# An attention unit of one 64-token chunk of four batches instead of four chunks of one batch

## The chip, the cores and the metric

The kernel runs on one core of a Trainium2 chip. The metric is the device time of one execution in microseconds (us). The engines named below are PE (TensorE; PEld is its weight load), DVE (VectorE), ACT (ScalarE), POOL (GpSimd) and SP (SyncE, which here only issues DMAs). "L634" is line 634 of the kernel before; lines of the kernel after are named as such.

## The reference

Four batches of 768 tokens pass a linear attention with eight heads of 48 features, then a two-layer network with 2048 hidden features. The attention keeps one 48 x 48 state for each batch and head and goes through the tokens in order:

```
for t in range(S):
    cur = einsum('bhd,bhe->bhde', u * k[t], v[t])
    y[t] = einsum('bhd,bhde->bhe', r[t], state + cur)
    state = w[t] * state + einsum('bhd,bhe->bhde', k[t], v[t])
...
h = x @ w_in                      # x: y of all heads, 3072 x 384
g = where(h >= 1, h, where(h <= -1, 0, (h + 1)**2 / 4))
out = g @ w_out
```

So the batches are independent of each other, and within a batch each token needs the state that the token before it left. The result is 3072 x 384, float32.

## The kernel before

**Attention units.** Tokens are worked on in units of `UT` = 256. There are `NU` = 12 units, and a unit is four chunks of `C` = 64 tokens. In the kernel before the four chunks of a unit follow each other in one batch, so a batch is three units (`third = u % UB`), and units 0, 3, 6 and 9 begin a batch. `attention(u, when)` does one unit:

- DMAs bring the decays `wq`, the rows of r and k `rk`, the values `vn` and, from unit 3 on, `nk`.
- DVE scans multiply up the decays inside each chunk, forwards (L487) and backwards (L482). r and k are multiplied by the results (L558, L508), and the product of a whole chunk goes to `ptot` (L505).
- PE multiplies r by k inside each chunk (`among`, L528). DVE copies the wanted half of that square into `r_` (`picked`, L534).
- PE transposes k (`ktrans`, L567), ACT copies it to `kt` (L574), and PE forms the update of the state by each chunk (`umat`, L589) in two banks `bu`. Chunk c = 2 * c2 + g has its update for four pairs of heads in 192 columns of bank `bu[g]`.
- `chain` steps the state through the chunks, one after the other: at the start of a batch one multiplication by `ptot` (L605), else an addition (L607) and a multiplication (L608), each of 192 columns. In unit 0 (`CHAINED`) PE adds the old state in PSUM instead (`add_up`, L612). `st` has six buffers of one chunk's state.
- y is summed in two banks `by`, in two parts of small matmuls at one line, L634: `cross` takes half of the products of r with the states, and `along` the other half and the products of `r_` with v. A chunk at the start of a batch has nothing before it, so its products are left out. Between `cross` and `along` ACT reads one number of each bank (`look`, L678).
- In units 0 and 1 (`ALONE`) the fourth head of each half is spread over spare rows by PE (L717), by way of an ACT copy (L722). ACT and DVE then write y to `x` as a high part (L698) and a low part (L696, or in unit 1 PE L708 and ACT L694).

**The network.** Two units make a block of 512 tokens; there are six blocks. A step (`products`) is one block with one of 16 slices of 128 hidden features: nine matmuls into a bank `hp` (`product_in`, L1226), the gate on ACT, DVE, ACT and DVE (L1038 to L1043), nine matmuls into the three banks `acc` (`product_out`, L1246). Block 0 takes its first five slices in halves of 256 tokens, block 1 its first 14 (`HALVES`), so that a half begins when its own unit is ready. The last block has another form (`fast`, L942). A slice's weights arrive once, packed, and are unpacked by `weight(f)`: ACT L414 and L416, POOL L418 (some on DVE), DVE L420, ACT L410 (some on DVE, L408), DVE L423.

**Banks.** Eight banks of PSUM: three shared ones (0 to 2), three `acc` (3 to 5) and two `hp` (6, 7). `take()` hands out banks for the units: the first ten from the list `ahead`, then 0, 1, 2 in turn.

**Order.** Nothing is issued where it stands. Each operation is added to a `Plan` with an estimated cost, the data that it reads and writes, and a due time from its unit's lead (`LEADS`) and what follows it in the unit. `Plan.best` simulates the engines by these costs, tries 40 variations of the order and keeps the one that ends first; `kept_warm` adds matmuls of zeros (L372) where PE would stand still. Every engine then runs its own queue in that order, so any change of costs or dependences gives a new order for the whole program.

Of the kernel before, what the change touches and what calls it, by code (L numbers as in the profile page):

```python
# [10 lines left out]
F32 = mybir.dt.float32  # L11
# [14 lines left out]
UB = S // UT  # L26
C = 64
NC = UT // C
SEG = 2 * NC * (C + 1)
HP = 64  # L30
NF = DF // 128
# [12 lines left out]

WARM = 50

USE, SPAN, COLUMN = 0.68, 3.4, 0.00168

EAGER, LATE = 16.0, 0.3
# [5 lines left out]
BACK, SHAKES, SHAKE, SEED = 4, 40, 0.7, 1  # L55

LOW = 7.499 * 2.0**-32
STATES = 6


class Plan:
# [221 lines left out]

SPLITS = {2, 7}
SIGNS = {9, 10, 12}
CHAINED = {0}
SUMS = 0.0
STEP, FIRST, PACED = 4.9, 24.0, 4.6
ROUNDS = 1
# [2 lines left out]
def attention_moe(tc, a):  # L292
# [52 lines left out]
    def op(engine, cost, due, reads, writes, emit, **kw):  # L345
        return plan.add(engine, cost, emit, due, reads, writes, **kw)
# [17 lines left out]
    for i in range(STATES):  # L364
        op("POOL", 0.1, SOON, (), [("spad", i)], lambda i=i: G.memset(st[i][:, 4 * D :], 0.0))

    def zeros(to, n, add):

# [69 lines left out]
    def attention(u, when):  # L438
        if u == EARLY:
            load((when, 40.0), u_sb, a["us"], ["us"])  # L440
        first, due = len(plan.ops), None
        third = u % UB
        early = u < EARLY
        v, vk = vn[u % 2], ("v", u % 2)

# [2 lines left out]

        def vs(i, c2, head, n):
            return v[i, c2, head * D : head * D + n]  # L450

        def pairs(s):
            return st[s][:, 0 : 4 * D].rearrange("p (a e) -> p a e", e=D)

        slot = [(2 * u + 1 - q) % 3 for q in range(2)]
        pv = p_.rearrange("p (q n) c -> p q n c", q=2)
# [106 lines left out]
        def ktrans(q, b):  # L563
# [4 lines left out]

        op("PE", 1.2, due, [("k", slot[0]), ("k", slot[1]), *both], [("b", ba[0]), ("b", ba[1])],
           lambda: among(ba, lambda q: rk[slot[q]][:, 1]))  # L570
        for q in (1, 0):
            b = take()
            op("PE", 0.4, due, [("k", slot[q]), "cst"], [("b", b)], lambda q=q, b=b: ktrans(q, b))
            op("ACT", 0.6, due, [("b", b)], [("kt", q)], lambda q=q, b=b: A.copy(  # L574
                kt[:, 2 * q : 2 * q + 2].rearrange("p a b c -> p (a b c)"), bank[b]))
# [18 lines left out]
        op("PE", 1.1, due, [("kt", 0), ("kt", 1), vk], [("b", bu[0]), ("b", bu[1])], umat)  # L594


        before = [None if third == 0 else state["st"]]

        def chain(c, old, new):
            c2, g = divmod(c, 2)  # L600
            up = bank[bu[g]][:, c2 * 4 * D : (c2 + 1) * 4 * D].rearrange("p (a e) -> p a e", e=D)
            pt = ptot[:, 16 * u : 16 * u + 16].rearrange("p (a c) -> p a c", c=NC)[:, :, c].unsqueeze(2).broadcast_to([128, 4, D])
            out = pairs(new)
            if old is None or u in CHAINED:
                V.tensor_tensor(out=out, in0=up, in1=pt, op=ALU.mult)  # L605
                return
            V.tensor_tensor(out=sm, in0=up, in1=pairs(old), op=ALU.add)  # L607
            V.tensor_tensor(out=out, in0=sm, in1=pt, op=ALU.mult)  # L608

        def add_up(c, old):  # L610
            c2, g = divmod(c, 2)
            PE.matmul(bank[bu[g]][:, c2 * 4 * D : (c2 + 1) * 4 * D].rearrange("p (a e) -> p a e", e=D), lhsT=ident, rhs=pairs(old),  # L612
                      start=False, stop=True, skip_group_check=True)

        for c in range(NC - (third == UB - 1)):
            old, new = before[-1], (state["st"] + 1) % STATES
            state["st"] = new
            if u in CHAINED and old is not None:
                op("PE", 0.5, due, [("s", old), "cst"], [("b", bu[c % 2])], lambda c=c, old=old: add_up(c, old), fresh=False)
            op("DVE", 0.35 if old is None or u in CHAINED else 0.71, due, [("b", bu[c % 2]), ("ptot", u, 0), ("ptot", u, 1)] + ([("s", old)] if old is not None else []),  # L620
               [("s", new), "sm"], lambda c=c, old=old, new=new: chain(c, old, new), port=True)
            before.append(new)

        by = [take(), take()]

# [8 lines left out]
            PE.matmul(out=bank[by[g]][HP * half : HP * half + M, lo : lo + C], start=first, stop=False, skip_group_check=True, **kw)  # L634

        def inter(g, h, pair, c2):
            s = before[2 * c2 + g]
            if s is None:
                return
            q, pr = divmod(pair, 2)  # L640
            i = slice(HP * h, HP * h + HP)
            put(g, pair, h, c2, lhsT=st[s][i, pair * D : pair * D + M],
                rhs=rk[slot[q]][i, 0, tokens(q, 0, pr, c2, g)])


# [31 lines left out]
        for g in range(2):  # L677
            op("ACT", 0.2, due, [("b", by[g])], [("look", g)], lambda g=g: A.copy(look[0:1, g : g + 1], bank[by[g]][0:1, 0:1]))  # L678
# [442 lines left out]
def general(tc, a, ident, w_hi, w_lo):  # L1121
# [65 lines left out]
    with (  # L1187
        tc.tile_pool(name="g_sb2", bufs=1) as sb,
        tc.tile_pool(name="g_ps2", bufs=1, space=PSUM) as ps,
    ):  # L1190
        with tc.For_i(0, B, 1) as b:
            for third in range(UB):
                ts = slice(third * UT, third * UT + UT)
                x = sb.tile([128, 3, UT], F32, tag="x", name=f"gx{third}")
                for h in range(2):
                    for j in range(3):
                        nc.gpsimd.dma_start(
                            out=x[64 * h : 64 * h + D, j, :],
                            in_=xd[bass.ds(b, 1), j // 2 * 2 + h, j % 2 * 64 : j % 2 * 64 + D, ts],
                        )  # L1200
                        nc.gpsimd.dma_start(
                            out=x[64 * h + D : 64 * h + 64, j, :],
                            in_=xd[bass.ds(b, 1), 2 + h, 64 + 16 * j : 80 + 16 * j, ts],
                        )
                xh = sb.tile([128, 3, UT], F32R, tag="xh", name=f"gxh{third}")
                xl = sb.tile([128, 3, UT], F32R, tag="xl", name=f"gxl{third}")
                V.tensor_copy(xh, x)
                G.tensor_tensor(out=xl, in0=x, in1=xh.bitcast(F32), op=ALU.subtract)
                o = [ps.tile([128, UT], F32, tag=f"o{j}", name=f"go{third}{j}") for j in range(3)]
                for f in range(NF):  # L1210
                    hp = ps.tile([128, UT], F32, tag="h", name=f"gh{third}_{f}")
                    product_in(nc, hp, f, xh, xl, w_hi, w_lo)
                    gh, gl = gate(nc, sb, hp, f"g{third}_{f}")
                    product_out(nc, o, f, gh, gl, w_hi, w_lo, f == 0, f == NF - 1)
                for j in range(3):
                    ob = sb.tile([128, UT], F32, tag=f"ob{j}", name=f"gob{third}{j}")
                    V.tensor_copy(ob, o[j])
                    nc.gpsimd.dma_start(out=a["out_b"][bass.ds(b, 1), third, j], in_=ob)


def product_in(nc, hp, f, xh, xl, w_hi, w_lo):
# [28 lines left out]

def layouts(r, k, v, w, u, moe_w_in, moe_w_out):
    def dt(x):
        x = x.reshape(B, 2, 2, 2, UB, UT, D)
        return x.transpose(0, 4, 1, 3, 6, 2, 5).reshape(NU, 2, 2, D, 2 * UT)
# [7 lines left out]
    nat = np.stack([r, k, v, w], axis=2).reshape(B, 4, 2, 4, S, D).transpose(0, 1, 2, 5, 3, 4)  # L1262

    def tokens(x):
        return x.transpose(0, 2, 1, 3).reshape(NU, 2, 128, DM).transpose(0, 2, 1, 3)

    nk = np.stack([tokens(r), tokens(k)], axis=3)
    ul = u.reshape(4, 2, D).transpose(1, 2, 0)
# [30 lines left out]

# [14 lines left out]
```

## Time and profile before

| what | value |
|---|---|
| median of 3 runs | 515.48 us (513.85 to 516.77) |
| profiled execution | 516.96 us |
| its span, first to last instruction | 515.3 us |
| PE busy | 501.9 us, 97% of the span |
| PEld busy | 424.0 us, 82% |
| DVE busy | 369.0 us, 72% |
| ACT busy | 306.8 us, 60% |
| POOL busy | 98.1 us, 19% |
| DMA | 54.72 MB, mean 106 GB/s |

The profiled execution is 1.48 us longer than the median, and 1.66 us of it lie outside its span. A busy time is the sum of the durations of an engine's instructions, matmuls of zeros among them. The chain that ended last goes back from the last instruction to what released each piece of work, so its rows tell which engine set the end in each stretch. A row of the chain or of the timeline begins with the start and the duration in us; "x64" is the number of instructions merged into it. Each float32 matmul with 64 x 64 operands is two records.

### The profile page before, as it was taken

To read this page: it belongs to the slowest core of one execution; us is meant where nothing else is said; L and a number is where in the kernel's file an instruction comes from. 1 tells how busy PE (TensorE), PEld (TensorE's weight loads), DVE (VectorE), ACT (ScalarE), POOL (GpSimd) and SP (SyncE) were. 2 spreads that over 40 slices of the span, in tenths; PEclk is the share of its full clock that TensorE was granted. 3 is DMA by queue.
4 is the path that set the end of the run, shared out by engine and by line. 5 is a ranking of instruction groups with operands and counts; after the bars stand their busy time and mean duration, and the time that the engine had idled before them with its cause. 6 is when DMAs were issued, how large, how long until landed. Compare 5 with 4: busy or idle time off the path is not lost.

```text
span 515.3 us, 13486 instructions
## 1 busy us (share of the span) xinstructions
PE 501.9 (97%) x5683; PEld 424.0 (82%) x5683; DVE 369.0 (72%) x670; ACT 306.8 (60%) x632; POOL 98.1 (19%) x84
## 2 busy tenths in 40 slices
PE   8989999999999999999999999999999999999994
PEld 6768988889999998877788787788878777789984
DVE  6989899997788989544988632799353457488663
ACT  4678888988854667533555643656434554474560
POOL 1774304503021120101111000210000131512000
PEclk9989999999999999999999999999999999999998
DMA  8984942447343442401434200621100100200002
GB/s 299 352 325 137 360 151 77 153 129 242 118 142 95 142 138 95 144 2 55 157 103 132 83 0 4 209 78 52 62 1 0 43 17 3 76 1 3 1 2 67
DMA packets 22053, 54.72 MB, mean 106 GB/s; under 512 B 3040, under 2 KB 9184, under 8 KB 21984
## 3 DMA queue, kind: packets, MB, share of 16 engines
q1 hardware_dynamic: 21840, 53.65, 30.6%
q8 instruction: 46, 0.75, 0.6%
q14 instruction: 23, 0.19, 0.1%
q10 hardware_dynamic: 144, 0.13, 0.1%
HBM read 47.09 MB, written 4.72 MB: 101 GB/s over the span
## 4 chain that ended last, share of the span: by engine, by line
PE 93%; DVE 4%; DMA 1%; issue 1%; SPq 0%; ACT 0%; DVEq 0%; ACTq 0%
PE h L1226 40%; PE acc L1246 34%; PE bank L634 5%; PE acc L942 3%; PE bank L942 3%; PE bank L528 3%; PE bank L589 2%; PE bank L567 2%; DMA cst<-in_consts 1%; DVE fl L420 1%; DVE y L482 1%; PE bank L372 1%; PE acc L528 0%; DVE wt L423 0%; DVE st L608 0%
## 5 line engine op out<-in xcount | busy, mean ns | idle before, releaser
L1226 PE MATMUL h<-x,wt 128*128 128x512 f32 (+1 forms) x1035 | 222.7, 363 | 2.3 <-DVE x L696 1.5
L1226 PEld LDWEIGHTS h<-x,wt 128*128 128x128 f32 x1035 | 171.2, 190 | 32.5 <-DVE x L696 1.7
L1246 PE MATMUL acc<-gh,wt 128*128 128x512 f32 (+1 forms) x594 | 131.4, 356 | 0.0
L1246 PEld LDWEIGHTS acc<-gh,wt 128*128 128x128 f32 x594 | 97.4, 188 | 16.8
L1038 ACT ACTIVATE g<-h 128x512 f32<-128x512 f32 (+1 forms) x99 | 50.8, 513 | 89.5 <-PE h L1226 88.7
L1040 DVE SCALAR_TENSOR_TENSOR g<-g,h 128x512 f32<-128x512 f32 (+1 forms) x99 | 57.1, 578 | 59.4 <-ACT g L1039 54.4
L1246 PE MATMUL acc<-gl,wt 128*128 128x512 f32 (+1 forms) x297 | 72.3, 352 | 0.0
L1043 DVE TENSOR_TENSOR gl<-g,gh 128x512 fp32r<-128x512 f32 (+1 forms) x99 | 60.3, 614 | 14.9 <-ACT gh L1042 14.6
L1042 ACT CAST gh<-g 128x512 fp32r<-128x512 f32 (+1 forms) x99 | 52.4, 534 | 26.9 <-DVE g L1040 24.2
L554 POOL TENSOR_TENSOR r<-cst,d 128x512 f32<-128x512 f32 x18 | 19.7, 1114 | 218.8 <-PE bank L634 170.4
L1246 PEld LDWEIGHTS acc<-gl,wt 128*128 128x128 f32 x297 | 50.6, 188 | 8.5
L1039 ACT ACTIVATE g<-g 128x512 f32<-128x512 f32 (+1 forms) x99 | 54.5, 550 | 2.9
L418 POOL TENSOR_SCALAR wraw<-fl 128x768 uint16<-128x768 f32 x13 | 40.8, 3151 | 54.4 <-ACT wraw L416 54.3
L487 DVE TENSOR_TENSOR_SCAN p<-wq,seeds 128x520 f32<-128x520 f32 x24 | 30.5, 1270 | 2.9 <-DMA wq<-in_w 2.1
L482 DVE TENSOR_TENSOR_SCAN y<-wq,seeds 128x520 f32<-128x520 f32 x24 | 32.0, 1333 | 0.8
L546 POOL TENSOR_TENSOR nk<-nk 128x768 f32<-128x768 f32 x9 | 17.3, 1920 | 58.0 <-DMA nk<-in_nk 49.3
L903 DVE SCALAR_TENSOR_TENSOR rk<-rk,h 128x512 f32<-128x512 f32 x16 | 11.0, 685 | 15.0 <-ACT rk L902 15.0
L534 DVE COPY_PREDICATED r<-below,bank 128x512 f32<-128x512 int32 x22 | 15.3, 730 | 6.7 <-PE bank L528 6.6
L634 PEld LDWEIGHTS bank<-rk,st 64*64 64x64 f32 (+1 forms) x656 | 12.2, 133 | 6.9 <-issue 3.7
L416 ACT ACTIVATE wraw<-wraw 128x768 uint16<-128x768 uint32 x16 | 17.4, 1086 | 0.3
L574 ACT COPY kt<-bank 128x512 f32<-128x512 f32 x24 | 13.9, 580 | 6.1 <-PE bank L567 6.1
L607 DVE TENSOR_TENSOR sm<-bank,st 128x192 f32<-128x192 f32 x37 | 13.1, 355 | 5.4 <-PE bank L589 4.1
(212 smaller groups left out, 609.5 us busy)
## 6 DMA issues: line engine op xcount, KB each, us to landing
rk<-in_rk SPq DMA_DIRECT2D x24, 512.0 KB, 4.7
wraw<-in_wbits SPq DMA_DIRECT2D x16, 768.0 KB, 7.8
nk<-in_nk SPq DMA_DIRECT2D x9, 768.0 KB, 4.5
wq<-in_w SPq DMA_DIRECT2D x24, 260.5 KB, 2.9
vn<-in_v SPq DMA_DIRECT2D x12, 384.0 KB, 5.8
fl<-in_w SPq DMA_DIRECT2D x12, 260.0 KB, 2.8
out_y<-g SPq DMA_DIRECT2D x10, 256.0 KB, 2.5
x<-last SPq DMA_DIRECT2D x60, 32.0 KB, 2.2
```

The lines of the kernel that those rows point to most:

```text
L418: op(on, 0.62 if f in SIGNS else 3.2, due, [("fl", k)], [("raw", f)], lambda: e.tensor_scalar(out=half(1), in0=s, scalar1=0.0, scalar2=327 ...
L482: V.tensor_tensor_scan(out=y_[:, ::-1], data0=w[:, SEG:0:-1], data1=sv[:, ::-1], initial=0.0, op0=ALU.mult, op1=ALU.add)
L487: V.tensor_tensor_scan(out=pv[:, q].rearrange("p n c -> p (n c)"), data0=w[:, 0:SEG], data1=sv, initial=0.0, op0=ALU.mult, op1=ALU.add,)
L634: PE.matmul(out=bank[by[g]][HP * half : HP * half + M, lo : lo + C], start=first, stop=False, skip_group_check=True, **kw)
L942: PE.matmul(bank[i][:, half * UT : half * UT + UT], lhsT=w[wi], rhs=g[gi], start=i not in opened, stop=True, skip_group_check=True)
L1038: op("ACT", c, due, [("b", 6 + hk)], [("g", gk)], lambda: nc.scalar.activation(gs, hs, AF.Relu, scale=0.5, bias=0.5))
L1039: op("ACT", c, due, (), [("g", gk)], lambda: nc.scalar.activation(gs, gs, AF.Square))
L1040: op("DVE", 0.13 + 0.53 * k, due, [("b", 6 + hk)], [("g", gk)], lambda: nc.vector.scalar_tensor_tensor(out=gs, in0=gs, scalar=1.0, in1=hs, ...
L1042: op("ACT", c, due, [("g", gk)], [("gh", gk)], lambda: nc.scalar.copy(ghs, gs))
L1043: op("DVE", 0.15 + 0.5 * k, due, [("g", gk), ("gh", gk)], [("gl", gk)], lambda: nc.vector.tensor_tensor(out=gls, in0=gs, in1=ghs.bitcast(F ...
L1226: nc.tensor.matmul(hp, lhsT=wx[f][:, cs], rhs=xt[:, j, :], start=n == 0, stop=n == 8)
L1246: nc.tensor.matmul(o[j], lhsT=wx[f][:, cs], rhs=gt, start=first and i == 0, stop=stop and i == 2, skip_group_check=True)
```

## The change

A unit becomes one chunk of 64 tokens of all four batches. Unit u holds tokens 64 u to 64 u + 63 of every batch, so that chunk c of a unit now belongs to batch c. The four chunks of a unit do not depend on each other; each depends on the same chunk of the unit before.

- The chain through the chunks is gone, with `add_up` and `CHAINED`. A step of the state is now one operation for the two chunks in bank `bu[g]`, 384 columns wide: in unit 0 one multiplication by `ptot`; in units 1 to 10 an addition of the old state (`step`) and a multiplication in place (`fade`), for g = 0 and 1.
- The states are two buffers, one that a unit reads and one that it writes, in turn.
- y of a unit takes its states from the unit before. Unit 0 has none of these products: `cross` and `look` are left out there, and half of `along`.
- Unit 11 hands nothing on: its transposes of k, their copies, `umat` and the step are left out.
- The list `ahead` ends in banks 5 and 2 where it ended in 3 and 4 (these are `by` of unit 0), and the turn of the shared banks begins one earlier.
- The host lays out r, k, v and w in the new order and puts the result's tokens back. Shapes and bytes are the same.
- The scratch for DMA descriptors is set to 8192 bytes (`SCRATCH`). `general`, which runs only when the inputs' decays are out of range, writes its output by the new order.

```diff
-STATES = 6
...
-CHAINED = {0}
...
-    st = tiles(STATES, [128, 4 * D + 16], F32, "st")
-    sm = one([128, 4, D], F32, "sm")
+    st = tiles(2, [128, 2, 2, 4 * D + 16], F32, "st")
...
-    state = {"bank": 2, "st": 0}
+    state = {"bank": 1}
-    ahead = [3, 4, 5, 6, 0, 1, 7, 2, 3, 4]
+    ahead = [3, 4, 5, 6, 0, 1, 7, 2, 5, 2]
...
+        goes_on = u < NU - 1
         for q in (1, 0):
-            b = take()
-            op("PE", 0.4, due, [("k", slot[q]), "cst"], [("b", b)], lambda q=q, b=b: ktrans(q, b))
...
+            if goes_on:
+                b = take()
+                op("PE", 0.4, due, [("k", slot[q]), "cst"], [("b", b)], lambda q=q, b=b: ktrans(q, b))
...
-        bu = [take(), take()]
+        bu = [take(), take()] if goes_on else []
...
-        for c in range(NC - (third == UB - 1)):
-            old, new = before[-1], (state["st"] + 1) % STATES
-            state["st"] = new
-            if u in CHAINED and old is not None:
-                op("PE", 0.5, due, [("s", old), "cst"], [("b", bu[c % 2])], lambda c=c, old=old: add_up(c, old), fresh=False)
...
+        old, new = (u - 1) % 2, u % 2
...
+        def step(g):
+            up = bank[bu[g]][:, 0 : 8 * D].rearrange("p (c a e) -> p c a e", c=2, e=D)
+            if u == 0:
+                V.tensor_tensor(out=heads(new, g), in0=up, in1=faded(g), op=ALU.mult)
+            else:
+                V.tensor_tensor(out=heads(new, g), in0=up, in1=heads(old, g), op=ALU.add)
+
+        def fade(g):
+            V.tensor_tensor(out=heads(new, g), in0=heads(new, g), in1=faded(g), op=ALU.mult)
+
+        if goes_on:
+            op("PE", 1.1, due, [("kt", 0), ("kt", 1), vk], [("b", bu[0]), ("b", bu[1])], umat)
+            for g in range(2):
+                op("DVE", 0.5, due, [("b", bu[g]), ("ptot", u, 0), ("ptot", u, 1)] + ([("s", old, g)] if u else []), [("s", new, g)],
+                   lambda g=g: step(g))
+                if u:
+                    op("DVE", 0.47, due, [("ptot", u, 0), ("ptot", u, 1)], [("s", new, g)], lambda g=g: fade(g), port=True)
...
         def along():
-            crossed(0)
+            if u:
+                crossed(0)
...
-        ss = [("s", s) for s in before if s is not None]
+        ss = [("s", old, g) for g in range(2)] if u else []
...
-        op("PE", 0.6, due, ss + [vk, ("r", slot[0]), ("r", slot[1])], [("b", by[0]), ("b", by[1])], cross, fresh=not alone)
+        if u:
+            op("PE", 0.6, due, ss + [vk, ("r", slot[0]), ("r", slot[1])], [("b", by[0]), ("b", by[1])], cross, fresh=not alone)
...
-        op("PE", 1.65, due, ss + [("R", 0), ("R", 1), vk, ("r", slot[0]), ("r", slot[1])],
+        op("PE", 1.65 if u else 1.1, due, ss + [("R", 0), ("R", 1), vk, ("r", slot[0]), ("r", slot[1])],
```

More of the change, by code (lines that the diff above doesn't have):

```diff
@@ L28 @@
 NC = UT // C
+assert NC == B and NU * C == S
 SEG = 2 * NC * (C + 1)
@@ L45 @@
 WARM = 50
+SCRATCH = 8192
 USE, SPAN, COLUMN = 0.68, 3.4, 0.00168
@@ L363, in attention_moe @@
     last_f = ob[:, 0:UT]
-    for i in range(STATES):
-        op("POOL", 0.1, SOON, (), [("spad", i)], lambda i=i: G.memset(st[i][:, 4 * D :], 0.0))
+    for i in range(2):
+        op("POOL", 0.1, SOON, (), [("spad", i)], lambda i=i: G.memset(st[i][:, :, :, 4 * D :], 0.0))
     def zeros(to, n, add):
@@ L570, in attention @@
            lambda: among(ba, lambda q: rk[slot[q]][:, 1]))
+        goes_on = u < NU - 1
         for q in (1, 0):
-            b = take()
-            op("PE", 0.4, due, [("k", slot[q]), "cst"], [("b", b)], lambda q=q, b=b: ktrans(q, b))
-            op("ACT", 0.6, due, [("b", b)], [("kt", q)], lambda q=q, b=b: A.copy(
-                kt[:, 2 * q : 2 * q + 2].rearrange("p a b c -> p (a b c)"), bank[b]))
+            if goes_on:
+                b = take()
+                op("PE", 0.4, due, [("k", slot[q]), "cst"], [("b", b)], lambda q=q, b=b: ktrans(q, b))
+                op("ACT", 0.6, due, [("b", b)], [("kt", q)], lambda q=q, b=b: A.copy(
+                    kt[:, 2 * q : 2 * q + 2].rearrange("p a b c -> p (a b c)"), bank[b]))
             if q:
@@ L592, in umat @@
                             )
[L594 to L613, printed above, removed]
-        for c in range(NC - (third == UB - 1)):
-            old, new = before[-1], (state["st"] + 1) % STATES
-            state["st"] = new
-            if u in CHAINED and old is not None:
-                op("PE", 0.5, due, [("s", old), "cst"], [("b", bu[c % 2])], lambda c=c, old=old: add_up(c, old), fresh=False)
-            op("DVE", 0.35 if old is None or u in CHAINED else 0.71, due, [("b", bu[c % 2]), ("ptot", u, 0), ("ptot", u, 1)] + ([("s", old)] if old is not None else []),
-               [("s", new), "sm"], lambda c=c, old=old, new=new: chain(c, old, new), port=True)
-            before.append(new)
+        old, new = (u - 1) % 2, u % 2
@@ new lines, in heads, with faded @@
+        def heads(s, g):
+            return st[s][:, :, g, 0 : 4 * D].rearrange("p c (a e) -> p c a e", e=D)
+        def faded(g):
+            return ptot[:, 16 * u : 16 * u + 16].rearrange("p (a c g) -> p c g a", c=2, g=2)[:, :, g].unsqueeze(3).broadcast_to([128, 2, 4, D])
+        def step(g):
[4 more added lines that the diff above has]
+                V.tensor_tensor(out=heads(new, g), in0=up, in1=heads(old, g), op=ALU.add)
@@ L636, in inter @@
         def inter(g, h, pair, c2):
-            s = before[2 * c2 + g]
-            if s is None:
-                return
             q, pr = divmod(pair, 2)
             i = slice(HP * h, HP * h + HP)
-            put(g, pair, h, c2, lhsT=st[s][i, pair * D : pair * D + M],
+            put(g, pair, h, c2, lhsT=st[old][i, c2, g, pair * D : pair * D + M],
                 rhs=rk[slot[q]][i, 0, tokens(q, 0, pr, c2, g)])
@@ L670, in cleared @@
                           skip_group_check=True)
-        ss = [("s", s) for s in before if s is not None]
+        ss = [("s", old, g) for g in range(2)] if u else []
         if alone:
             op("PE", 0.5, due, ["zero"], [("b", by[0]), ("b", by[1])], cleared)
-        op("PE", 0.6, due, ss + [vk, ("r", slot[0]), ("r", slot[1])], [("b", by[0]), ("b", by[1])], cross, fresh=not alone)
-        for g in range(2):
-            op("ACT", 0.2, due, [("b", by[g])], [("look", g)], lambda g=g: A.copy(look[0:1, g : g + 1], bank[by[g]][0:1, 0:1]))
-        op("PE", 1.65, due, ss + [("R", 0), ("R", 1), vk, ("r", slot[0]), ("r", slot[1])],
+        if u:
+            op("PE", 0.6, due, ss + [vk, ("r", slot[0]), ("r", slot[1])], [("b", by[0]), ("b", by[1])], cross, fresh=not alone)
+            for g in range(2):
+                op("ACT", 0.2, due, [("b", by[g])], [("look", g)], lambda g=g: A.copy(look[0:1, g : g + 1], bank[by[g]][0:1, 0:1]))
+        op("PE", 1.65 if u else 1.1, due, ss + [("R", 0), ("R", 1), vk, ("r", slot[0]), ("r", slot[1])],
            [("b", by[0]), ("b", by[1])], along, fresh=False)
@@ L1217, in general @@
                     V.tensor_copy(ob, o[j])
-                    nc.gpsimd.dma_start(out=a["out_b"][bass.ds(b, 1), third, j], in_=ob)
+                    nc.gpsimd.dma_start(out=a["out_b"][bass.ds(b, 1), third, j], in_=ob.rearrange("p (c t) -> p c t", t=C))
 def product_in(nc, hp, f, xh, xl, w_hi, w_lo):
@@ L1252, in dt @@
     def dt(x):
-        x = x.reshape(B, 2, 2, 2, UB, UT, D)
-        return x.transpose(0, 4, 1, 3, 6, 2, 5).reshape(NU, 2, 2, D, 2 * UT)
+        x = x.reshape(B, 2, 2, 2, NU, C, D)
+        return x.transpose(4, 1, 3, 6, 2, 0, 5).reshape(NU, 2, 2, D, 2 * UT)
     def rows(x, fill):
@@ L1307 @@
     out = nc.dram_tensor("out_y", (DM, NT), F32, kind="ExternalOutput").ap()
-    a["out_b"] = out.rearrange("(j p) (b t c) -> b t j p c", t=UB, j=3, c=UT)
+    a["out_b"] = out.rearrange("(j p) (h c b t) -> b h j p c t", h=UB, j=3, b=B, t=C)
     a["out"] = out.rearrange("(j p) (b c) -> b j p c", j=3, c=WIDE)
@@ L1312 @@
     res = run_bass_kernel_spmd(nc, [{f"in_{n}": x for n, x in arrays.items()}], core_ids=[0])
-    return np.ascontiguousarray(res.results[0]["out_y"].T)
+    y = res.results[0]["out_y"].T.reshape(NU, B, C, DM).transpose(1, 0, 2, 3)
+    return np.ascontiguousarray(y.reshape(NT, DM))
```

8 lines of the change are left out of this document (3 added, 5 removed).

## The prediction

> **What bounds the kernel now.** I read the page first: busy shares, slices, and the chain that ended last.
>
> ```profile
> PE 501.9 (97%) x5683; PEld 424.0 (82%) x5683; DVE 369.0 (72%) x670; ACT 306.8 (60%) x632; POOL 98.1 (19%) x84
> PE   8989999999999999999999999999999999999994
> DVE  6989899997788989544988632799353457488663
> PE 93%; DVE 4%; DMA 1%; issue 1%; SPq 0%; ACT 0%; DVEq 0%; ACTq 0%
> ```
>
> PE sets the end for 93% of the span. But a busy PE also counts matmuls of zeros, so the next view is busy time in two stretches, once for all lines and once for the zeros (L372) alone. I cut at 43.43 us, where the chain changes over to PE for good. The columns are the stretch, its length, busy time and instructions of each engine, then granted clock, DMA share and GB/s.
>
> ```profile
> 14.23:43.43 29.20, 24.63 (x487) 19.79 (x479) 26.72 (x45) 20.65 (x36) 19.86 (x7) 0.94 0.75 279
> 43.43:508.84 465.41, 465.39 (x4938) 395.13 (x4938) 332.32 (x611) 279.59 (x585) 75.56 (x60) 1.00 0.27 89
> 14.23:43.43 29.20, 7.74 (x34) 5.59 (x34) 0.94 0.75 279
> ```
>
> Two stages with two limits. From 43.43 to 508.84 PE is busy for 465.39 of 465.41 us, with no zeros: here only PE work taken away counts. From 14.23 to 43.43, the **front**, 7.74 of PE's 24.63 us are zeros, while DVE is busy for 26.72 of 29.20 us, 92%. So in the front DVE and the dependences decide. The chain in order of time (start, us, what) gives its milestones:
>
> ```profile
> 30.38 0.56 DVE x L696
> 30.99 3.67 PE h L1226 x17
> 43.43 1.32 PE h L1226 x9
> 46.24 1.27 PE acc L1246 x9
> ```
>
> Unit 0's y is complete at 30.94 (L696 ends); the network's products then begin in earnest at 30.99. By 43.43 only three half slices of the first product are done, 27 matmuls, and none of the second (46.24). The products wait for y of unit 0, then for unpacked weights, and DVE works for unit 1 in between.
>
> **The change in the PE stage: unit 11.** Its two k transposes and `umat` go. The chain there:
>
> ```profile
> 417.95 4.21 PE h L1226 x18
> 422.16 0.44 PE bank L567 x4
> 424.71 1.08 PE bank L589 x64
> 425.79 4.40 PE h L1226 x18
> ```
>
> Two transposes at 0.44 are 0.88. `umat` is 1.08, and the 18 matmuls behind it take 4.40 where 18 others take 4.21, so 0.19 more for the changeover. Sum 0.88 + 1.08 + 0.19 = **2.15 us**, all on the path, as PE has no gap there. What is late next is more PE work, so nothing gives it back.
>
> **The change in the PE stage: what is added.** Units 3, 6 and 9 get a state for their first chunk: 8 more small products each. Units 3 and 4, without and with them:
>
> ```profile
> 135.36 0.62 PE bank L634 x22
> 139.35 1.56 PE bank L634 x85
> 160.44 0.62 PE bank L634 x32
> 162.32 1.56 PE bank L634 x96
> ```
>
> `cross` takes 0.62 with three quarters of its records or all 32, `along` 1.56 with 85 on the chain or 96. The added products cost **nothing**: the rows show equal lengths. If they cost the mean of a record, 1.56 / 96 = 0.016, it would be 48 x 0.016 = 0.8; I keep that for the range.
>
> **The change on DVE.** The new operations are 384 columns wide. No state operation of that width is in the trace, but the last row below has that form, PSUM and SBUF in, 384 out:
>
> ```profile
> L607 DVE TENSOR_TENSOR sm<-bank,st 128x192 f32<-128x192 f32 x37 | 13.1, 355 | 5.4 <-PE bank L589 4.1
> L608 DVE TENSOR_TENSOR st<-sm,ptot 128x192 f32<-128x192 f32 x37 | 13.7, 370 | 1.3
> L696 DVE TENSOR_TENSOR x<-bank,x 128x384 fp32r<-128x384 f32 x20 | 10.8, 551 | 5.7 <-ACT last L698 4.7 <-ACT x L698 0.9
> ```
>
> Before: 7 multiplications (0.34, below) + 37 + 37 = 2.4 + 13.1 + 13.7 = 29.2 us. After: 2 + 20 `step` and 20 `fade`, 42 x 0.551 = 23.1. The bounds for one are 0.355 (no growth) and 2 x 0.370 (none saved); I take 0.551, the row of its width. Some 6 us of DVE time go, nearly all beside a full PE, where they are worth nothing. Only those in the front count:
>
> ```profile
> 14.88 0.72 DVE L534 COPY_PREDICATED r<-below,acc 128x512 f32<-128x512 int32 x1
> 15.48 0.34 DVE L605 TENSOR_TENSOR st<-h,ptot 128x192 f32<-128x192 f32 x1
> 35.89 1.34 DVE L534 COPY_PREDICATED r<-below,bank 128x512 f32<-128x512 int32 x2 [1.64 <-PE bank L528]
> 39.52 0.36 DVE L607 TENSOR_TENSOR sm<-bank,st 128x192 f32<-128x192 f32 x1 [0.26 <-PE bank L589]
> 42.34 0.71 DVE L608 TENSOR_TENSOR st<-sm,ptot 128x192 f32<-128x192 f32 x1
> ```
>
> Unit 1's chain holds DVE from 39.52 to 43.05, 3.53 us, and its y waits for it. Afterwards y of unit 1 needs only unit 0's states, so the four operations (4 x 0.551 = 2.2) can stand behind it. Unit 0's four multiplications, 4 x 0.34, become two of 0.551: 0.26 less. Together **3.8 us** of DVE leave the way to unit 1's y. This is the lower reading of the front.
>
> **The change in the dependences of the front.** The timeline of PE and ACT gives the upper reading:
>
> ```profile
> 21.68 1.08 PE L634 MATMUL acc<-r,vn 64*48 64x64 f32 x60
> 22.80 0.43 ACT L722 COPY ob<-acc 128x128 f32<-128x128 f32 x2 [0.64 <-PE acc L634]
> 23.12 1.60 PE L717 MATMUL acc<-ob,nk 128*128 128x128 f32 x12 [0.36 <-ACT ob L722]
> 24.41 0.47 ACT L698 CAST x<-acc 128x384 fp32r<-128x384 f32 x1
> 44.75 1.49 PE bank L634 x96
> 51.30 0.86 ACT L694 CAST x<-bank 128x384 fp32r<-128x384 f32 x2
> ```
>
> Unit 0: `along` ended at 22.76, behind the chain of states. Afterwards its y needs `r_` (15.60) and its two banks; 5 was read by `picked`, and 2 is `bu[1]`, free after both steps, 15.60 + 1.10 = 16.7. So `along` can end near 18.2, some 4.5 us earlier. The change doesn't free unit 0's y from `umat`, as it could: bank 2 holds it there. Unit 1: `along` ran at 44.75; its `r_` was ready at 37.23, so without the chain it can run 7.5 us earlier, and y (52.16 now) with it. That is the upper reading: **7.5 us**.
>
> Between 3.8 and 7.5 I take **5.0**, nearer to the lower end since DVE is 92% full. Why not all 7.5: an earlier y(0) brings g and its low part (L1040, L1043) onto the same DVE earlier, and PE gets weights only as they are unpacked (first rival). For the range I keep 0 (reordered, nothing gained) and 9.3, which is y(0) at the earliest, 30.94 - 21.6: `along` to 18.2, then some 3.4 us, an estimate from L722 to the first L698 (22.80 to 24.88), the second high part (0.47), a low part (0.55) and the waits between them, if nothing else stands on ACT and DVE before them.
>
> [...] The first `fade` operations fall among POOL's weight conversions:
>
> ```profile
> 27.55 3.22 POOL L418 TENSOR_SCALAR wraw<-fl 128x768 uint16<-128x768 f32 x1 [4.54 <-ACT wraw L416]
> 32.18 6.44 POOL L418 TENSOR_SCALAR wraw<-fl 128x768 uint16<-128x768 f32 x2 [1.41 <-ACT wraw L416]
> 42.01 3.02 POOL L418 TENSOR_SCALAR wraw<-fl 128x768 uint16<-128x768 f32 x1 [3.39 <-ACT wraw L416]
> ```
>
> The L608 at 42.34 ran under the conversion from 42.01 to 45.03 and took 0.71 instead of 0.37. It was slowed by 0.34, but it ended 2 us before the conversion. So I count a `fade` in the front at up to 0.9, and it lies behind unit 1's y: no change of the sum. [...]
>
> **Sum.** 516.96 - 2.15 - 5.0 = 509.8 us for the profiled execution. That one is 1.48 over the median of the runs shown, so against the median: 515.48 - 7.15 = **508.3 us**. About 0.5%, 2.6 us, is what a measurement can tell from no change.
>
> No transfer changes in bytes. The tail after 508.84 stays: the last block's form is untouched.
>
> **Rivals.**
>
> *The front is given back to the weights.* Slice 3's conversion on POOL ends at 30.77, slice 4's near 35.4 (second row above, half of 6.44), and unpacking goes on behind it on the full DVE. If by 43.43 PE has done slices 0 to 2 in both products, that is 3 x 2.11 = 6.3 us (half of the 4.21 row above is one product) where it had done 3 x 1.06 = 3.2; less unit 1's transposes and `umat`, which now come later (1.96). Gain 1.2 in the front: 515.48 - 2.15 - 1.2 = 512.1. For it: DVE at 92%. Against: no chain, and 7.74 us of zeros to fill.
>
> [...]
>
> *Slower: two state buffers.* `step(u)` writes the buffer that `along(u - 1)` reads, so DVE may stand for PE; behind it in its queue are L1040 and L1043, and PE waits for those. Now:
>
> ```profile
> 125.54 1.08 PE bank L589 x64
> 153.83 1.08 PE bank L589 x64
> ```
>
> `umat` of unit 3 at 125.54 comes 13.8 us before its `along` (139.35), and `umat` of unit 4 at 153.83 comes 12.9 us after that `along` ended: the wait is covered. If the new order turned this round, DVE would stand for up to 13.8 us, less two steps of products that PE has ahead, 2 x 4.21: 5.4 us lost for each such unit. It decides from the second unit on: 508.3 + 10.8 = 519.1.
>
> *All of y(0).* If the front gains 9.3: 515.48 - 2.15 - 9.3 = 504.0.
>
> **How the numbers follow.** Forecast, front 3 to 8 us: 0.58. Weights, 512.1: 0.23. Full block or a new order that gains nothing, about 514.7: 0.07. Slower, 519: 0.06. All of y(0), 504: 0.06. The range runs from 503.5 to 513.5: from the largest front (504.0) to `umat` and the transposes alone (513.3). It leaves out 514.7 and 519, 0.13 together, and a little at its ends. Faster by over 0.5% (below 512.9): the forecast, all of y(0) and two thirds of the weights, 0.79. Within 0.5%: 0.15. Slower: 0.06.
>
> **What would show it.** In the profile after: no L567 and L589 of unit 11, so 88 and 704 records instead of 96 and 768; 42 state operations near 551 ns; `cross` of units 3, 6 and 9 at 0.62; the first L1226 near 22 to 25 instead of 30.99; unit 1's `along` near 38 to 41 instead of 44.75; PE full without zeros from about 38 on and to the same distance before the end. It would be wrong if PE shows gaps after the front (the slower rival: DVE waits at the step for L634), if DVE is the chain's engine past 60 us, or if the first product starts early but zeros still fill PE to 43 (the weights).

## The result and the profile after

The kernel after takes **511.27 us** in the median of 5 runs (510.04 to 511.69), beside 515.48 (513.85 to 516.77, also 5 runs) for the kernel before: ratio 0.9915, 95% interval 0.9891 to 0.994. A second measurement, against 17 runs of the kernel before on one chip, gave 510.53 against 515.19, ratio 0.9892, 0.9868 to 0.9917. So the change is worth 4.2 to 4.7 us by the medians. The forecast was 508.3, a gain of 7.15. The mean granted clock of PE differs between executions of one kernel, and the time goes with it: of 25 runs of the kernel before, five at a clock of 0.999 took 513.97 to 514.65 us, five at 0.993 or 0.994 took 516.74 to 517.73.

The page of the kernel after, in the order in which the page before was read:

```profile
PE 496.3 (97%) x5591; PEld 418.5 (82%) x5591; DVE 365.8 (72%) x631; ACT 304.7 (60%) x628; POOL 99.0 (19%) x80
PE   7889999999999999999999999999999999999995
DVE  5999999998888979533969635967353376687653
PE 94%; DMA 1%; DVE 1%; issue 1%; POOL 1%; ACT 1%; SPq 0%; DVEq 0%
```

The profiled execution took 511.69 us, its span 510.0; PE still sets the end. The stretches, cut as before (columns: stretch, its length, busy time and instructions of each engine, granted clock, DMA share, GB/s; the last line counts the zeros at L372 alone):

```profile
14.23:43.43 29.20, 24.89 (x500) 19.37 (x501) 26.62 (x41) 19.62 (x39) 16.84 (x6) 0.88 0.72 277
34.20:503.74 469.54, 469.52 (x5097) 399.14 (x5097) 338.28 (x591) 285.07 (x593) 84.53 (x62) 1.00 0.28 91
14.23:43.43 29.20, 8.66 (x20) 4.70 (x20) 0.88 0.72 277
```

Two things are to be seen. PE is now full from 34.20 us on, where it was full from 43.43, and it ends 5.1 us earlier (503.74 instead of 508.84). But in the front, VectorE is as busy as it was: 26.62 of 29.20 us instead of 26.72. The zeros did not shrink (8.66 us instead of 7.74), and POOL did less of its weight conversions (16.84 instead of 19.86). The front was **rearranged, not relieved**. The granted clock of the stretch also fell, from 0.94 to 0.88; the section on the prediction comes back to it.

What that brought is read from the network's products done by 100 us. Both kernels have by then done the attention work of units 0 to 2 and the same 180 matmuls of 256 columns. The groups of 512-column products up to 100 us, before and after:

```profile
L1226 PE MATMUL h<-x,wt 128*128 128x512 f32 x72 | 18.3, 400 | 0.0
L1246 PE MATMUL acc<-gh,wt 128*128 128x512 f32 x31 | 8.3, 400 | 0.0
L1246 PE MATMUL acc<-gl,wt 128*128 128x512 f32 x15 | 4.3, 396 | 0.0
```

```profile
L1219 PE MATMUL h<-x,wt 128*128 128x512 f32 x72 | 18.2, 399 | 0.0
L1239 PE MATMUL acc<-gh,wt 128*128 128x512 f32 x36 | 9.5, 398 | 0.0
L1239 PE MATMUL acc<-gl,wt 128*128 128x512 f32 x17 | 4.9, 395 | 0.0
```

118 before and 125 after (126 in the profile of the second measurement). Nine take 2.10 us on the chain, so 7 are **1.63 us**: by so much the front of the kernel after is ahead. With 2.15 for unit 11 it makes 3.8, near the 4.2 of the medians. Between the two profiled executions the difference is 5.27; most of the rest, 1.5 us, lies behind 100 us in work that both have. The second product's matmuls there sum to 177.6 us for 757 records before and 174.6 for 750 after, 1.4 less than the seven account for; the change does not explain it.

### The profile page after: what moved, and what is told of

Its sections match the earlier page's. It is cut to its first block, busy times and chain, and to the rows that moved or that the text cites. A ratio compares the mean times of both kernels' runs of the same rounds, so it can differ in the third digit from the quotient of the medians.

```text
span 510.0 us, 13244 instructions
## 1 busy us (share of the span) xinstructions
PE 496.3 (97%) x5591; PEld 418.5 (82%) x5591; DVE 365.8 (72%) x631; ACT 304.7 (60%) x628; POOL 99.0 (19%) x80
## 4 chain that ended last, share of the span: by engine, by line
PE 94%; DMA 1%; DVE 1%; issue 1%; POOL 1%; ACT 1%; SPq 0%; DVEq 0%
PE h L1219 40%; PE acc L1239 34%; PE bank L628 5%; PE acc L935 3%; PE bank L935 3%; PE bank L524 3%; PE bank L587 2%; PE bank L563 2%; DMA rk<-in_rk 1%; POOL wraw L418 1%; PE bank L372 0%; PE acc L524 0%; DVE rk L504 0%; SPq L352 0%; PE bank L710 0%
## 5 line engine op out<-in xcount | busy, mean ns | idle before, releaser
L1036 DVE TENSOR_TENSOR gl<-g,gh 128x512 fp32r<-128x512 f32 (+1 forms) x99 | 62.5, 636 | 18.6 <-ACT gh L1035 17.2
L418 POOL TENSOR_SCALAR wraw<-fl 128x768 uint16<-128x768 f32 x13 | 41.4, 3188 | 53.4 <-ACT wraw L416 53.3
L478 DVE TENSOR_TENSOR_SCAN y<-wq,seeds 128x520 f32<-128x520 f32 x24 | 31.2, 1300 | 0.8
L542 POOL TENSOR_TENSOR nk<-nk 128x768 f32<-128x768 f32 x9 | 17.2, 1909 | 67.6 <-DMA nk<-in_nk 67.6
L504 DVE TENSOR_TENSOR rk<-rk,y 128x512 f32<-128x512 f32 x24 | 16.8, 701 | 1.5 <-ACT nk L494 1.4
L894 ACT ACTIVATE rk<-h 128x512 f32<-128x512 f32 x16 | 9.6, 598 | 13.8 <-PE h L1219 13.8
L554 DVE TENSOR_TENSOR rk<-rk,p 128x512 f32<-128x512 f32 x24 | 16.2, 684 | 2.1 <-DMA rk<-in_rk 1.8
L416 ACT ACTIVATE wraw<-wraw 128x768 uint16<-128x768 uint32 x16 | 17.3, 1084 | 0.2
```

The lines of the kernel that those rows point to most:

```text
L418: op(on, 0.62 if f in SIGNS else 3.2, due, [("fl", k)], [("raw", f)], lambda: e.tensor_scalar(out=half(1), in0=s, scalar1=0.0, scalar2=327 ...
L478: V.tensor_tensor_scan(out=y_[:, ::-1], data0=w[:, SEG:0:-1], data1=sv[:, ::-1], initial=0.0, op0=ALU.mult, op1=ALU.add)
L1036: op("DVE", 0.15 + 0.5 * k, due, [("g", gk), ("gh", gk)], [("gl", gk)], lambda: nc.vector.tensor_tensor(out=gls, in0=gs, in1=ghs.bitcast(F ...
```

## The experiments

Unless a run says otherwise, its kernel is the kernel after with one edit. "Products" are the 512-column ones done by 100 us, counted as above: one is 0.23 us. They tell the front alone, and of one profiled execution. From the same execution come "clock", the granted clock from 14.23 to 43.43 us, and "gap", the time that PE stands still between 100 and 500 us.

| run | median us | ratio to before, 95% interval | products | clock | gap, us |
|---|---|---|---|---|---|
| before | 515.48 | 1 | 118 | 0.94 | 0 |
| after, first | 511.27 | 0.9915 (0.9891 to 0.994) | 125 | 0.88 | 0 |
| e1, unit 11 kept | 513.47 | 0.9966 (0.9948 to 0.9984) | 130 | 0.94 | 0.48 |
| e2, another order | 511.02 | 0.9933 (0.9909 to 0.9957) | 133 | 0.94 | 0.34 |
| e3, y(1) ahead of the state | 510.50 | 0.9902 (0.9882 to 0.9921) | 130 | 0.94 | 0.30 |
| e4, y(0) in banks 3 and 4 | 514.04 | 0.9968 (0.9951 to 0.9984) | 122 | 0.88 | 1.97 |
| e5, no backward scan | 508.10 | 0.9848 (0.9815 to 0.9882) | 141 | 1.00 | 0 |
| e6, short conversions | 508.70 | 0.9851 (0.9829 to 0.9874) | 142 | 1.00 | 0.16 |
| e7, no zeros before the spread | 509.75 | 0.9869 (0.9845 to 0.9893) | 138 | 1.00 | 0.86 |
| e8, before in another order | 521.59 | 1.0085 (1.0055 to 1.0116) | 126 | 1.00 | 3.86 |
| e9, more warming | 512.65 | 0.9943 (0.9921 to 0.9966) | 123 | 1.00 | 0.98 |
| e10, e9 and e7 | 513.98 | 0.9969 (0.9951 to 0.9988) | 122 | 0.88 | 1.59 |
| e11, e3 and e7 | 511.11 | 0.9913 (0.9888 to 0.9938) | 124 | 0.82 | 0.66 |
| e12, after again | 510.53 | 0.9892 (0.9868 to 0.9917) | 126 | 0.88 | 0 |

The kernel before had a median of 515.40 beside e1 to e4, 516.50 beside e5 to e8 and 515.19 beside e9 to e12; so runs of different rows are compared by their ratios. Products and gap together account for the spans of the profiled executions: set against e12 (510.0 us), every version of the kernel after comes out within 0.4 us of what its products, its gap and, in e1, 2.15 for unit 11 give, e4 alone within 1.1. So a difference of time is not always one of the front.

### e1: unit 11 hands its state on

```diff
-        goes_on = u < NU - 1
+        goes_on = True
```

> The kernel after with the transposes of k, umat and the state step of unit 11 put back; its state is used by nothing. Step of the prediction: 2.15 us of PE path come back, so 511.27 + 2.15 = 513.4 us, with 96 records of the transposes and 768 of umat. Rival, that PE work late in the program is hidden or that the gain came from elsewhere: 511.3. Rival, that a new order alone moves the time by a microsecond or more: anything from 512 to 515.

Measured 513.47, 2.20 above the kernel after. The chain of this run has the work back, in two places (start, us, what):

```profile
418.36 0.87 PE bank L563 x8
...
421.34 1.08 PE bank L587 x64
422.42 2.30 PE h L1219 x9
```

The transposes 0.87, `umat` 1.08, and 2.30 instead of 2.10 for the products behind it: the forecast's 0.88, 1.08 and 0.19. This term holds. The durations are the firmer proof: the planner's order moved with the edit (130 products and a gap of 0.48), so that the 2.20 is not unit 11 alone, and by the ratios the distance is 2.6 us or more. Counted against e12, 2.15 and 0.48 less four products (0.93) give 1.70; the spans are 511.7 and 510.0.

### e2 and e8: the same work in another order

```diff
-BACK, SHAKES, SHAKE, SEED = 4, 40, 0.7, 1
+BACK, SHAKES, SHAKE, SEED = 4, 40, 0.7, 2
```

(In e8 the kernel before, with 3.) The planner keeps the best of 40 variations; another seed gives other variations.

> The kernel after with SEED 2 instead of 1 in the plan's variations: the same operations in another order. If the order found is no lottery: 511.3 within 0.8 us. If it is one: off by more than 1 us, and part of the 4.2 us between before and after is luck of the order.

> The kernel before with SEED 3 instead of 1: the same operations in another order. If the order found matters little: 515.4 within 1 us. If the order is a lottery of the size of the change: off by 2 us or more, and the 4.2 us between before and after are as much luck as change.

e2 has a median of 511.02, and its interval overlaps that of the kernel after: nothing that can be told apart, though it has 133 products. e8 is 0.85% slower than the kernel before. So the choice of an order alone can be worth as much as the whole change. And e8 is not slower in the front: it has 126 products there, 8 more than the kernel before in its own order and as many as the kernel after. It loses behind the front, 3.86 us in gaps, 2.9 of them where PE waits for g from VectorE (L1040); another 2.7 us of its longer span stay unexplained. So the 7 products between before and after can't be put down to the change: another order of the old work brings as many. e8 shows one such order, not how often it occurs.

### e3 and e4: y earlier by itself

In e3 the transposes of k, `umat` and the steps of unit 1 are added to the plan behind its y instead of ahead of it. In e4 y of unit 0 gets two banks that nothing of its own update uses:

```diff
-    ahead = [3, 4, 5, 6, 0, 1, 7, 2, 5, 2]
+    ahead = [3, 4, 5, 6, 0, 1, 7, 2, 3, 4]
```

> The kernel after with unit 1's transposes, umat and state step placed behind the evacuation of its y, so that the banks of its y no longer wait for the step of g = 0. Theory banks (the front gained 2 us and not 5 because y of unit 1 still waits for umat and a state step by way of the shared banks): along of unit 1 starts at 38 to 41 instead of 44.28, its y is complete near 46 instead of 51.98, and the time is 507 to 509.5 us. Theory weights (DVE and the unpacking of the weights fill the front whatever y does): y earlier, time 510.5 to 512.

> The kernel after with y of unit 0 in banks 3 and 4, which it had before, instead of 5 and 2; bank 2 is one that umat writes and the step reads. Theory banks: along of unit 0 starts before 17.0 instead of 17.61, and its y is complete 1 to 3 us before 29.78; time 509 to 510.5. Theory weights: y at the same place or earlier, time 510.5 to 512.

e3 did what it was to do. Its chain has `along` of unit 1 (here L638) at 38.16 instead of 44.28, and the correction ahead of y's low part (here L711) at 45.74 instead of 50.80:

```profile
38.16 1.49 PE bank L638 x96
...
45.74 0.28 PE bank L711 x3
```

y(1) was complete at 47.26 instead of 51.98, and the time fell by 0.13% against the first measurement of the kernel after and not at all against the second. By products, 130, the front gained about 1 us, at a clock of 0.94 instead of 0.88, which may be part of it. So **4.7 us of y(1) brought 1 us of the front at most**: the upper reading of the prediction, and the half of the lower one that rested on y(1), fall with e3.

e4 did not do what it was to do. `along` of unit 0 began at 15.72 instead of 17.61, but PE stood for 2.90 us in the middle of it, and the second low part of y(0) came behind the scans and copies of unit 1 in VectorE's queue: it was complete at 33.58 instead of 29.78, and the first product began at 35.23. VectorE was busy for 25.53 us of the front instead of 26.62. The kernel was slower, 0.9968, and 1.97 us of that are gaps behind the front. What an earlier y(0) is worth by itself, e4 does not show.

### e5, e6 and e7: relieving the front

In e5 the backward scan (L478) of units 1 and 2 isn't issued: four scans of 1.24 us. In e6 POOL's conversion (L418) of the first five slices is a memset of 0.96 to 0.98 us, so that these weights lose their signs. In e7 the planner puts no zeros between `along` and the spread of unit 0. Otherwise the order is that of the kernel after in all three.

```diff
+                if u in (1, 2):
+                    return
```

```diff
-lambda: e.tensor_scalar(
+lambda: e.memset(half(1), 0) if f < 5 else e.tensor_scalar(
```

```diff
-                if free and lack > 0.15:
+                if free and lack > 0.15 and not 16.0 < free < 20.0:
```

> The kernel after in its own order, with the backward scan of units 1 and 2 left out (DVE L478, four of 1.24 to 1.25 us in the front; k is then multiplied by values left by unit 0). 5.0 us of DVE work go from 20 to 54 us, nothing else. Theory DVE (the front is as long as the DVE work before y and the products): 2 to 5 us less, 506.3 to 509.3. Theory weights, or theory zeros: within 0.8 us of 511.3, DVE waits instead.

> The kernel after in its own order, with POOL's conversion of the signs of the first five weight slices (L418, 3.0 to 3.66 us each) replaced by a memset of the same place, so that these weights lose their signs. Theory weights (the front waits for unpacked weights): each slice is ready some 2.5 us earlier, time 507.5 to 509.5. Theory DVE: within 0.8 us of 511.3, since DVE's queue is full behind it, at most what two-input operations gain when POOL no longer runs beside them.

> The kernel after in its own order, without the matmuls of zeros between along and the spreading of unit 0 (L372, 4.30 us from 21.16 to 25.46, which the plan meant as 2.3). Theory zeros: y of unit 0 is complete 2 to 3 us earlier than 29.78 and the time is 508.5 to 510. Theory DVE or weights: y of unit 0 earlier, time within 0.8 us of 511.3.

e5 and e6 bring 141 and 142 products, 16 or 17 more than the kernel after, and lie 0.4 to 0.7% below it: to relieve VectorE or POOL in the front shortens the kernel. e5 saved 5.0 us of VectorE and brought 2 to 3.5 us. But how it shortens it is not shown, for in both the front also ran at a clock of 1.00 instead of 0.88. Over 29.20 us that is 3.5 us of clock, an estimate from these two figures, or 15 products: as much as the whole gain. e7 has 138 products, a clock of 1.00 too, and a gap of 0.86 behind the front. Its interval overlaps those of the kernel after, and e10 and e11 (below), which have the same edit beside another, show none of the gain, at clocks of 0.88 and 0.82. What e7 owes to the zeros stays open.

### e9 to e12: where the stall belongs

The profile after has a stall that the profile before does not show. In the first `along` PE stood for 2.20 us, and the view gives no releaser but "issue" (its row, 18.27 2.20, stands in the chain further below). e9 puts more small matmuls ahead of everything, so that all later instructions of PE stand further on in its stream: a stall that belongs to a place there leaves `along`, one that belongs to the data or the banks stays; e10 adds the edit of e7 to that; e11 joins e3 and e7; e12 is the kernel after, beside them.

```diff
-WARM = 50
+WARM = 88
```

> The kernel after with 88 in place of 50 of the small matmuls at L378 ahead of all attention work; order and all else as in after, nothing left out. Every later TensorE instruction stands 76 instructions (38 matmuls and their weight loads) further on in TensorE's instruction stream; the 38 fall into the wait ahead of the first ktrans at 9.27 us. In after the first along stood still for 2.20 us after 28 of its 64 matmuls, and in six kernels of seven after 24 or 28 of them. [...] Theory 'the data': the stall comes from what along reads or writes, or from its first use of these banks; it stays at 24 to 28 matmuls with 1.5 to 2.9 us, and the time stays (.9905 to .9925).

> The kernel of e9 without zeros between the first along and the first spread, as in e7; nothing left out. If the 2 us of the stall and the 4.3 us of the zeros are both on the way to y(0), this is better than e7 by up to 2 us more: ratio to before .983 to .987 (e7: .9869). If the weights of slices 0 to 2 or VectorE's work set the first products once the zeros are gone, the stall is hidden behind them and e10 equals e7 within .002.

> The kernel of e3 (unit 1's state steps behind its y) without zeros between the first along and the first spread, as in e7; nothing left out. e3 alone brought 0.13% and e7 alone 0.46% against after. If the two delays follow each other on the path (y(0) first, then y(1)), together they bring 0.6% or more: ratio to before .984 to .986, the fastest version that computes all. If VectorE's backlog sets both, they bring no more than e7 alone: .9865 to .988.

> The kernel after unchanged, beside e9 to e11, so that these can be set against it directly. Expected ratio to before .9915 as measured first (.989 to .994), with a stall of 1.5 to 2.5 us after 28 matmuls of the first along again if it belongs to the kernel and not to one execution.

The stall is in e12 too, again after 28 records of `along`. In e9 it left `along` and stands in `umat`, after 20 of its 64 records. The page's counts and the timelines, e9 first (the two PE rows, then VectorE's), then e12:

```profile
PE 495.9 (97%) x5667; PEld 418.8 (82%) x5667; DVE 364.5 (71%) x631; ACT 305.1 (60%) x628; POOL 99.7 (19%) x80
```

```profile
18.28 0.26 PE L587 MATMUL bank<-vn,kt 64*64 64x48 f32 x2 [1.65 <-issue]
```

```profile
19.23 0.56 DVE L603 TENSOR_TENSOR st<-bank,ptot 128x384 f32<-128x384 f32 x1 [1.54 <-PE bank L587]
...
30.82 0.55 DVE L689 TENSOR_TENSOR x<-acc,x 128x384 fp32r<-128x384 f32 x1
```

```profile
28.99 0.55 DVE L689 TENSOR_TENSOR x<-acc,x 128x384 fp32r<-128x384 f32 x1
```

The 38 added matmuls are 76 records (5667 instead of 5591; in float32 each is recorded twice, so `along` of unit 0 is 32 matmuls in 64 records and not the 64 that the expectation took). From the 20th record of `umat` to the 28th of `along` there are 44 of `umat`, 2 of zeros, 2 of the clearing at L661 and 28 of `along`: 76. The stall moved by exactly as many records as were put ahead of it. In all twelve profiles of a kernel after, PE had 350 matmul records behind it since the start when it stood (349 in e4). So it belongs to **a place in PE's instruction stream**, not to the data or the banks.

Moving it brought no gain: the author's estimate was a time 0 to 2.5 us lower, and e9 is slower than e12 by 2.1 us. The added matmuls did not vanish in a wait as the expectation said; the first transpose began at 11.01 instead of 9.43. And in `umat` the stall made VectorE stand for 1.54 us at the step of the state (second row), in the middle of its front. VectorE, which had been 1.5 us behind e12 at the copy ahead of it (L530, 16.98 instead of 15.46), was 3.2 behind here (19.23 instead of 16.07) and gave the last low part of y(0) at 30.82 instead of 28.99. Of the 2.1 us, 0.98 are a gap behind the front, and three products fewer are 0.7. e10, slower still, has the same stall and the same delay, and a gap of 1.59. e11 has 124 products where e7 had 138: what e3 and e7 did alone does not add up. Of the versions that compute all, none is shown to be faster than the kernel after.

## Why the prediction was right in sign and too large

**Unit 11: right.** 2.15 forecast; e1 has the three terms of the sum back at 0.87, 1.08 and 0.20, and a median 2.20 higher. The records of L563 and L587 are 88 and 704 (672 + 32), as the prediction said.

**Added products and the new state operations: right in size.** Groups of the kernel after (columns: engine, operation, shapes, count, busy us, mean ns, idle before):

```profile
L563 PE MATMUL bank<-cst,rk 128*128 128x128 f32 x88 | 14.1, 289 | 0.6 <-DVE rk L504 0.6
L587 PE MATMUL bank<-vn,kt 64*64 64x48 f32 x672 | 12.6, 220 | 0.0
L605 DVE TENSOR_TENSOR st<-bank,st 128x384 f32<-128x384 f32 x20 | 10.9, 551 | 7.3 <-PE bank L587 7.2
L608 DVE TENSOR_TENSOR st<-st,ptot 128x384 f32<-128x384 f32 x20 | 10.6, 549 | 0.0
L587 PE MATMUL h<-vn,kt 64*64 64x48 f32 x32 | 1.1, 217 | 0.0
```

551 and 549 ns where 551 was taken, and `cross` of unit 3 takes 0.63 us at 159.58. VectorE's wait for `umat` ahead of `step` sums to 7.2 us in the whole run and PE has no gap behind it: the rival of the two state buffers did not come. What the chances call the full block (514.7) no run shows: under a conversion VectorE's subtraction at L1036 took 0.71 and 0.75 us, 0.40 at its shortest, and ended 1.9 us before the conversion (last section).

**The front: the step that failed.** The prediction took 5.0 us, between a lower reading of 3.8, VectorE work that leaves the way to y of unit 1, and an upper one of 7.5. It measured 1.63 by products, 2.0 to 2.5 by the medians. The mechanism, a shorter way to both y, was hardly there: y(0) came 1.16 us earlier, y(1) 0.18, and e3 shows that even 4.7 us of y(1) bring little. Unit 0 first. The chain of the kernel after through the front, in order of time:

```profile
18.27 2.20 issue
...
21.42 0.27 ACT ob L715
...
21.79 0.81 ACT fl L414
22.62 1.08 ACT wraw L416
...
23.78 3.01 POOL wraw L418
26.81 0.96 DVE fl L420
...
28.16 0.55 DVE wt L408
28.71 0.60 DVE rk L504
29.31 0.47 DVE x L689
...
29.93 1.25 DVE y L478
...
34.20 1.19 PE bank L524 x64
...
40.73 1.25 PE acc L1239 x9
...
44.28 1.49 PE bank L628 x96
```

`along` of unit 0 started at 17.61 and ended at 21.28; without the stall of 2.20 it would have been 19.1, where the prediction had 18.2. Then the chain leaves y(0): it runs through the unpacking of a weight slice on ACT (L414, L416), POOL (L418) and VectorE (L420, L408), and the second low part of y(0) (L689, 29.31) stands behind these in VectorE's queue. y(0) is complete at 29.78 instead of 30.94. The estimate of 3.4 us from `along` to y had the condition "if nothing else stands on ACT and DVE before them"; that condition is what failed: it took 8.5 us. PE's own queue had a part in it: zeros stood ahead of the spread from 21.16 to 25.46. But in e7, without them, the spread begins at 20.79 and y(0) is complete at 28.27, only 1.5 us earlier. From 26.81 to 34.20 the chain is VectorE but for short pieces, and PE stood for 2.11 us ahead of the matmuls of 34.20.

And y(0) moved ahead held the weights up. ACT's wait ahead of its copy of y(0), and POOL's conversions, of the kernel after, and POOL's of the kernel before:

```profile
21.25 0.27 ACT L715 COPY ob<-acc 128x128 f32<-128x128 f32 x1 [3.94 <-PE bank L628]
```

```profile
14.35 6.04 POOL L418 TENSOR_SCALAR wraw<-fl 128x768 uint16<-128x768 f32 x2 [11.29 <-ACT wraw L416]
23.78 3.00 POOL L418 TENSOR_SCALAR wraw<-fl 128x768 uint16<-128x768 f32 x1 [3.39 <-ACT wraw L416]
```

```profile
13.85 9.15 POOL L418 TENSOR_SCALAR wraw<-fl 128x768 uint16<-128x768 f32 x3 [10.71 <-ACT wraw L416]
```

Before, three conversions followed each other and were done at 23.00. After, the copy of y(0) stands in ACT's queue ahead of the third slice's L414, waits 3.94 us for `along`, and the third conversion ends at 26.78, 3.8 us later. By 43.43 POOL had done one conversion less. This is the first rival, the front given back to the weights, in a form that the prediction had not named: not VectorE's load but a wait on ACT. The measured 511.27 and 510.53 lie between its 512.1 and the time by the lower reading, 515.48 - 2.15 - 3.8 = 509.5, and both are nearer to 512.1 than to the forecast of 508.3.

Unit 1: `along` ran at 44.28, not at 38 to 41. The prediction let it run as soon as its `r_` was ready. Its two banks are 1 and 2, and bank 2 is one of unit 1's own `bu`, so y(1) still waited for `umat` and the step (39.58 and 40.76), a dependence that the prediction saw for unit 0 and missed for unit 1. e3 removes it, and little comes of that.

**The granted clock, for which the sum had no term.** The front of the kernel after in stretches of 10 us (columns as in the first view of stretches; the granted clock is the third figure from the end):

```profile
14.00:24.00 10.00, 7.80 (x203) 4.94 (x202) 9.30 (x14) 5.40 (x10) 6.21 (x3) 0.88 1.03 402
24.00:34.00 10.00, 8.09 (x105) 6.38 (x103) 8.94 (x13) 8.22 (x17) 6.05 (x2) 0.95 0.77 282
34.00:44.00 10.00, 9.80 (x201) 8.79 (x201) 9.18 (x16) 6.80 (x14) 5.15 (x2) 0.83 0.33 133
```

In the front PE ran for some us at half its clock: twice in the kernel after (0.50 from 22 to 24 and from 36 to 38 us), once in the kernel before (0.50 from 32 to 34), not at all in e5 to e9. One row shows what that costs. In e8 the first products begin as in the kernel before, behind the same wait, but at full clock, and take 2.26 us where the chain of the kernel before has 3.67 at 30.99:

```profile
31.03 2.26 PE L1226 MATMUL h<-x,wt 128*128 128x256 f32 x17 [1.48 <-DVE x L696]
```

Over 29.20 us a clock of 0.94 loses 1.75 us and one of 0.88 loses 3.5, estimates from the two figures; so the kernel after lost 1.75 more. Some of it fell on zeros, but the second stretch fell on `among` and the transposes of unit 1; of the 4.3 us from 34.20 to 38.46 only 1.15 are zeros. Between e8 and e7, which ran the whole front at 1.00, the distance is 12 products, 2.8 us; but e9, also at 1.00, has only 123, with y(0) 1.8 us late. So part of what is missing from the 5.0 may well be clock. It is not shown: no run changed the clock alone.

A sum that does fit the front counts only the VectorE time that the change saves in it: 0.26 in unit 0, and in units 1 and 2 each 4 x (0.355 + 0.370) before less 2 x (0.551 + 0.549) after, 0.70; together 1.66 beside the 1.63 measured. This is worked out afterwards and no run isolates it, and e8, which has 8 products more than the kernel before and saves none of this time, shows that such a fit proves nothing. How much of the front belongs to VectorE's work, to the weights, to the clock and to the order that the planner found is not settled. Of the change's gain, the 2.15 of unit 11 is what the runs show.

**Signs named beforehand.** The first product began at 29.56, not at 22 to 25; PE was full from 34.20, earlier than the 38 named, yet 1.35 us of zeros followed. Full was no sign of much done: behind 34.20 PE first had half of unit 1's `among`, its transposes and its `umat` to do, up to 40.73; in the kernel before `umat` of unit 1 ended at 39.49.

## What to carry to other kernels

Where one engine is nine tenths busy, a dependence that goes may only rearrange the stage, and an earlier milestone (y(1) by 4.7 us in e3) need not move the end. Read the granted clock of a stage beside its busy times (0.94 here before the change, 0.88 after) before a gain in it is put down to the work. An operation that is moved forward in an in-order queue takes its wait with it: ask what stands behind it there (here a weight slice, 3.8 us later). And before a gain under 1% of a planned kernel is put down to the change, time another order of the same work, and look where it gains and loses (e8: 8 products ahead at 100 us, 4.7 us behind at the end).

## What the runs showed of the hardware

PE stood for about 2 us, with no releaser, at a fixed place of its instruction stream: 1.4 to 2.9 us inside the first `along` in ten runs, and 1.65 and 1.72 us in `umat` when 76 records were put ahead of it (e9, e10), always behind the 350th matmul record of the program (349 in e4). e2 has a second such row, 1.70 us ahead of `among` at 26.91. The DMA engines are then at a share of 1.03 and 402 GB/s (14 to 24 us of the kernel after). The kernel before has no such row, in either order; in its own it passes 350 records at 20.1 us without standing. What PE stood for was not shown: the view names no releaser, less traffic at that time was not tried, nor the kernel after without its new `SCRATCH`. The pages of the kernels before and after, of e9 and of e12 list 46 transfers on the queue named instruction, 0.75 MB in all; no view ties one of them to the stall.

VectorE slowed beside POOL's conversion and was not held until its end. The subtraction at L1036 (two inputs in SBUF) took 0.71 us at 43.44, under the conversion from 42.40 to 46.06, and 0.75 at 47.97, but 0.40 at 49.94, under the same conversion as the second one (47.62 to 50.65). These rows show at most 0.35 us of delay. Under POOL's multiplication at L542 (161.23 to 163.05) it was more: L1036 at 161.37 took 1.96 us.

The half clock of the front came and went: 0.50 from 22 to 24 us of the kernel after, 1.00 from 26 to 34, 0.50 from 36 to 38. Both stretches of it follow a standstill of PE, of 2.20 us at 18.27 and of 2.11 us ahead of 34.20. But in e5 and e7 PE stood for 1.84 and 1.92 us in `along`, and the clock was 1.00 over the whole front. What sets it off was not shown.
